# Bucketed attention with a one-expert router: pattern products placed ahead of the value products, the cross moves in the third key-tile step, the router's scratch in the common PSUM pool

## The chip, the cores and the metric

The kernel runs on one core of a Trainium2 chip. The metric is the device time of one execution in microseconds (us); lower is better. Five engines work side by side, each through its own list of instructions in order: TensorE (PE) multiplies matrices into PSUM, VectorE (DVE) and ScalarE (ACT) read PSUM and SBUF, GpSimd (POOL) works on SBUF, and SyncE (SP) issues DMA transfers. Engines wait for each other by semaphores. An instruction that waits holds up all that stands behind it on its engine.

## The reference, cut to what matters

```python
# q, k, v: 4 batches x 8 heads x 768 x 64; proj: 64 x 6
q_bits, k_bits = (q @ proj > 0), (k @ proj > 0)            # 6 bits = one of 64 buckets
mask   = bucket(q_bits)[:, None] == bucket(k_bits)[None, :]
scores = where(mask, q @ k.T / 8, -1e9)
attn   = exp(scores - rowmax); attn /= rowsum + 1e-9
x      = (attn @ v) laid out as 3072 tokens x 512
# router: 8 experts, top 1
logits = x @ w_gate + modality_bias[modality_id]
e_idx  = argmax(logits); gate_w = softmax(logits)[e_idx]
out[tokens of e] = gate_w * (relu(x @ w1[e]) @ w2[e])       # 512 -> 1024 -> 512
```

All of it is float32.

## The kernel before

The 32 heads are taken as 16 pairs, four pairs to a batch. A pair has 768 queries and 768 keys, so six key tiles of 128. The attention part fills the first 475 us or so; the expert GEMMs come after it and are not touched.

For one pair i, PE does this. Scores (L295, L296: two products per tile, a high and a low part) go to one of two banks `pss`; ACT takes their exponentials into `pb` (L307 for 512 columns of one head, L314 for the last 256 of both). POOL adds the `pb` tiles up in `sp` (L317) for the row sums. The value products (L341, opened by L336) multiply `pb` by `vt` into two banks `psu`, 16 products for two key tiles in a block; ACT copies the result to `ut` (L346). Beside this PE works ahead: for pair i+1 it computes the maximum over the matching keys (L239, L245 into one of two banks `psm`, reduced by DVE in L241, L247, then L255 and ACT's L257 `nm`, transposed by L264 and folded in by DVE in L266, L267); for pair i+2 it prepares the operands, `prep`: turn and split the inputs (hx on ACT, L176 on DVE and POOL, moves by DMA in L159), the sign bits (L202), two cross moves (`cross`, L159), and four pattern products (L222). A pattern product is 128x384 into one of two banks `psx`; ACT empties it in two instructions, L223 and L224. `psx` is also the bank for the transposes, the row sums (L359), the batch's gathering (`finish`, `finish_x`) and the router.

The order of PE and of SP is written by hand. For each pair the six strings of PLAN are gone through, one for each key tile, letter by letter: S is one score step, M one step of the maxima, T the next step of prep(i+2), P a last step that is left over from the pair before, A the value products of one key tile, B the transposes of `nm`, V and Q small sums, L and l the loads of `xt` and `vt`. Small letters besides, and F, G, E, take pieces of the batch's `finish` (with the router, `route`), of `finish_x` and of the scatters, each in certain pairs only (FIN). Pair 0 has its own strings (PLAN0, FIRST). The order on ACT, DVE and POOL is set by a scheduler.

PSUM has eight banks: two each of psx, psm, pss and psu. The second psu bank needs only 256 of its 512 columns for the value products; its right half is the scratch of the router (`Spots`, at L400 to L630 and L655 to L705: logits, differences, one-hot weights, ranks, and what the early slots of the experts are worked out in). `route` runs in pieces behind `finish`: logits and maximum; one-hot `oh`; the count products (L617, `tri` and `onesb` by `oh`), ranks, positions. UPTO says how many pieces of the third batch's `finish` run ahead of `early_slots`.

Of the kernel before, what the change touches and what calls it, by code (L numbers as in the profile page):

```python
# [28 lines left out]
P = 128  # L29
# [4 lines left out]
RELIEF = ()  # L34
UPTO = 12
PLAN = (
    "LvSPMSMSfMTfexyhk",
    "SMSMVfSMAAQTesyghk",
    "SMTSMSMlGwEfxyk",
    "SMTSMSMAAFwGwEekk",  # L40
    "SMSMTSMgwfExeshk",
    "SMTSMTSMBAABFGFfFfggehksk",
)
# [35 lines left out]

class Spots:  # L80

    psum = None

    def __call__(self, pool, shape, name, at):
        if self.psum is None:
            return pool.tile(shape, F32, name=name)
        n = int(np.prod(shape[1:]))
        ap = self.psum[:, at:at + n]
        return ap if len(shape) == 2 else ap.rearrange("p (a e) -> p a e", a=shape[1])


def attention(ctx, actx, tc, a, x_d, route, setup, early_slots, early_tables, latest, adds, bias, later, spot):
    nc = tc.nc
# [16 lines left out]
    sm = actx.enter_context(tc.tile_pool(name="sm", bufs=4))  # L110
# [4 lines left out]
    ps_u = actx.enter_context(tc.tile_pool(name="ps_u", bufs=1, space=PSUM))  # L115
    shared = ps_u.tile([P, MAIN], F32, name="psu1")
    spot.psum = shared[:, REST:MAIN]

# [17 lines left out]
    ident = fconst.tile([P, P], F32, name="ident")  # L136
# [192 lines left out]
    def weigh():  # L329

        for i in range(NPR):
            t = st[i]
            t["u"] = [ps_u.tile([P, MAIN], F32, name="psu0"), shared[:, 0:REST]]
            for part in range(2):
                w = COLS[part].stop - COLS[part].start
                nc.tensor.matmul(t["u"][part][:, 0:w], vsb[i % 2], t["lone"][:, COLS[part]], start=True, stop=False, skip_group_check=True)  # L336
            for kt in range(NT):
                for part in range(2):
                    w = COLS[part].stop - COLS[part].start
                    for h in range(2):  # L340
# [25 lines left out]
    def finish(b):  # L366
# [26 lines left out]
        for w in range(2):  # L393
            n = 4 if w == 0 else 2
# [6 lines left out]
            yield  # L401
        lg = spot(bp, [P, NT, 8], "lg", 0)
        nc.vector.tensor_reduce(out=lg, in_=gl.rearrange("p t h e -> p t e h"), axis=AX.X, op=ALU.add)
        yield
        yield from route(b, lg, ps_x)

# [42 lines left out]
    with tc.manual_schedule(engines={mybir.EngineType.PE, mybir.EngineType.SP}):  # L449
# [67 lines left out]
        sums(NPR - 1)  # L517
        spot.psum = None
    return finish, finish_x, ps_x, ident


# [27 lines left out]
def router(ctx, tc, a, x_d, tab):  # L549
# [45 lines left out]

    scattered, latest, adds, later, counts, spot = [], [], [], [], [], Spots()

    def route(b, lg, ps):
        l = lg
        m = wk.tile([P, NT], F32, name="rm")  # L600
        nc.vector.tensor_reduce(out=m, in_=l, axis=AX.X, op=ALU.max)
        d = spot(wk, [P, NT, E], "rd", 48)
        nc.vector.tensor_tensor(out=d, in0=l, in1=m.unsqueeze(2).broadcast_to([P, NT, E]), op=ALU.subtract)
        ex = wk.tile([P, NT, E], F32, name="rex")
        nc.scalar.activation(ex, d, AF.Exp)
        yield
        w = spot(wk, [P, NT, E], "rw", 96)
        nc.vector.scalar_tensor_tensor(out=w, in0=d, scalar=0.0, in1=rev.unsqueeze(1).broadcast_to([P, NT, E]), op0=ALU.is_ge, op1=ALU.mult)
# [3 lines left out]
        nc.vector.tensor_tensor(out=oh, in0=w, in1=wm.unsqueeze(2).broadcast_to([P, NT, E]), op=ALU.is_equal)  # L612
        yield
        pp = ps.tile([P, HALF], F32, name="psx")
# [7 lines left out]
        if b == EARLYB - 1:  # L622
            counts.append(spot(wk, [P, E], "counts", 200))
            nc.vector.tensor_tensor(out=counts[0], in0=run[b % 2], in1=pp[:, 64:64 + E], op=ALU.add)
        nc.vector.tensor_tensor(out=run[(b + 1) % 2], in0=run[b % 2], in1=pp[:, 64:64 + E], op=ALU.add)
        yield
        rec = recs[:, b]
        sm = spot(wk, [P, NT], "rsum", 192)
# [3 lines left out]
        yield  # L632
        nc.vector.tensor_tensor(out=rk, in0=rk, in1=oh, op=ALU.mult)
        pos = spot(wk, [P, NT], "pos", 192)
        nc.vector.tensor_reduce(out=pos, in_=rk, axis=AX.X, op=ALU.add)
        posi = wk.tile([P, NT], I32, name="posi", bufs=2)
        nc.vector.tensor_copy(out=posi, in_=pos)
        yield
# [19 lines left out]
    def above(cnt, row, name):  # L658
        g = spot(wk, [P, E, 12], "sg", 0)
        nc.vector.tensor_tensor(out=g, in0=cnt.unsqueeze(2).broadcast_to([P, E, 12]), in1=step[:, row], op=ALU.is_gt)  # L660
        nb = spot(wk, [P, E], name, 208)
        nc.vector.tensor_reduce(out=nb, in_=g, axis=AX.X, op=ALU.add)
        return nb

    def cumulate(nb, name):
        c2 = spot(wk, [P, E, E], "sc2", 96)
        nc.vector.tensor_tensor(out=c2, in0=low, in1=nb.unsqueeze(1).broadcast_to([P, E, E]), op=ALU.mult)
        cu = spot(wk, [P, E], name, 216)
        nc.vector.tensor_reduce(out=cu, in_=c2, axis=AX.X, op=ALU.add)
        cx = spot(wk, [P, E], name + "x", 224)  # L670
        cs = cu
        if spot.psum is not None:
            cs = wk.tile([P, E], F32, name=name + "s")
            nc.vector.tensor_reduce(out=cs, in_=c2, axis=AX.X, op=ALU.add)
        nc.vector.tensor_tensor(out=cx, in0=cs, in1=nb, op=ALU.subtract)
        return cu, cx

    def assign(n, cu, cx, first, size, out):

        sel = spot(wk, [P, n, E], f"sel{n}", 160)  # L680
        sl = slot[:, 0:n].unsqueeze(2).broadcast_to([P, n, E])
# [4 lines left out]
        nc.vector.tensor_tensor(out=t, in0=sel, in1=eid.unsqueeze(1).broadcast_to([P, n, E]), op=ALU.mult)  # L686
        r = spot(wk, [P, n], f"selr{n}", 192)
# [3 lines left out]
        w = spot(wk, [P, E], "selw", 232)  # L691
        if size:
# [15 lines left out]
    def early_slots():  # L708
        nb = above(counts[0], 0, "enb")
# [298 lines left out]
def body(tc, a, out):  # L1008
# [47 lines left out]
```

## Time and profile before

| | us |
|---|---|
| median of three runs | 790.35 (789.85 to 791.34) |
| the profiled execution | 790.72 |
| its span (first to last instruction) | 788.9 |
| PE busy | 747.6 (95%) |
| DVE busy | 477.8 (61%) |
| POOL busy | 445.6 (56%) |
| ACT busy | 414.8 (53%) |

The profiled execution's own time lies 1.8 us above its span and 0.4 us above the median. The clock that TensorE was granted was in the highest tenth in all of the 40 slices of the profile page. Busy shares are means over two unlike stages, so what a wait costs is to be read in its own stage. A row of the trace gives the start, the duration and, in brackets, the time that the engine sat idle before it and what it waited for.

### The profile page before, as it was taken

Reading aid. Unit: us, or ns where it says so; the run is one execution under the profiler, and the core shown is the slowest. Engines: PE = TensorE matmul, PEld = TensorE weight load, DVE = VectorE, ACT = ScalarE, POOL = GpSimd, SP = SyncE. Lnnn points to the kernel's source line nnn. Section 1 sums busy time; section 2 is a strip of 40 time slices with the busy share of each in tenths; the row PEclk is TensorE's granted clock in tenths of the full one; section 3 lists DMA queues with packets and bytes.
Section 4 is the critical chain, followed back from the end, with each engine's and each line's share of the span. In section 5 each row is a group of like instructions: output and inputs, shape, how many; then the busy total and the mean of one; then the engine's idle time right before and its main releaser. Section 6 shows DMA issues by size and latency. Waiting matters only on the chain.

```text
span 788.9 us, 11622 instructions
## 1 busy us (share of the span) xinstructions
PE 747.6 (95%) x4060; PEld 520.3 (66%) x4060; DVE 477.8 (61%) x829; ACT 414.8 (53%) x732; POOL 445.6 (56%) x325
## 2 busy tenths in 40 slices
PE   5899999999999999999998999999999999999996
PEld 2565566555656566665555546878888888888885
DVE  5777677577777768767766667744344343742422
ACT  3666576666557566666554455333243334643423
POOL 7398988788779888879885982123220204302002
PEclk9999999999999999999999999999999999999999
DMA  6665554264346434454400737376443435844411
GB/s 195 153 189 160 160 130 131 62 160 114 104 126 183 101 97 113 118 170 121 121 22 28 138 77 265 122 126 200 141 139 103 149 105 182 287 117 134 120 55 61
DMA packets 59573, 104.11 MB, mean 132 GB/s; under 512 B 9709, under 2 KB 30957, under 8 KB 59504
## 3 DMA queue, kind: packets, MB, share of 16 engines
q1 hardware_dynamic: 53424, 88.10, 41.0%
q0 software_dynamic: 4928, 13.14, 5.1%
q10 hardware_dynamic: 1152, 2.03, 0.9%
q8 instruction: 34, 0.56, 0.3%
q14 instruction: 35, 0.29, 0.1%
HBM read 59.76 MB, written 13.33 MB: 93 GB/s over the span
## 4 chain that ended last, share of the span: by engine, by line
PE 65%; DVE 11%; issue 10%; ACT 5%; DMA 4%; POOL 3%; SPq 1%; POOLq 0%; ACTq 0%; DVEq 0%
PE psu L341 12%; PE pss L295 8%; PE pss L296 6%; PE hps L846 4%; PE hps L848 4%; PE hps L847 4%; PE yps L892 4%; PE yps L890 4%; PE yps L891 4%; PE psm L239 4%; PE psm L245 2%; ACT pb L307 2%; DVE b_1g L176 2%; PE psx L359 1%; DVE a_0g L266 1%
## 5 line engine op out<-in xcount | busy, mean ns | idle before, releaser
L317 POOL TENSOR_TENSOR sp<-sp,pb 128x768 f32<-128x768 f32 x124 | 233.2, 1908 | 40.5 <-ACT pb L314 37.2
L307 ACT ACTIVATE pb<-pss 128x512 f32<-128x512 f32 x192 | 114.4, 598 | 112.8 <-PE pss L296 96.6
L241 DVE TENSOR_REDUCE mx<-psm 128x1 f32<-128x512 f32 x192 | 130.6, 687 | 55.8 <-PE psm L239 54.8
L341 PE MATMUL psu<-pb,vt 128*64 128x512 f32 (+1 forms) x768 | 136.8, 497 | 4.9 <-DVE eslot L703 2.6
L799 DVE TENSOR_TENSOR w<-raw,w 128x1024 fp32r<-128x1024 f32 x64 | 79.5, 1249 | 94.8 <-ACT w L797 77.2
L797 ACT CAST w<-raw 128x1024 fp32r<-128x1024 f32 x64 | 66.9, 1050 | 73.9 <-PE yps L892 62.7
L341 PEld LDWEIGHTS psu<-pb,vt 128*64 128x64 f32 x768 | 50.9, 138 | 76.2 <-issue 56.4
L817 POOL DMA_INDIRECT xg<-x_d,tb x18 | 22.5, 1248 | 117.8 <-DMA tb<-tab 113.5
L295 PE MATMUL pss<-a_0g 128*128 128x512 f32 x192 | 80.3, 418 | 2.6 <-ACT pb L307 1.7
L890 PE MATMUL yps<-w,hl 128*128 128x512 f32 x208 | 82.7, 398 | 0.0
L892 PE MATMUL yps<-w,hh 128*128 128x512 f32 x208 | 81.3, 391 | 0.0
L891 PE MATMUL yps<-w,hh 128*128 128x512 f32 x208 | 80.9, 389 | 0.0
L846 PE MATMUL hps<-xh,w 128*128 128x512 f32 x192 | 75.6, 394 | 0.8 <-DVE hl L853 0.8
L847 PE MATMUL hps<-xl,w 128*128 128x512 f32 x192 | 74.9, 390 | 0.1
L848 PE MATMUL hps<-xh,w 128*128 128x512 f32 x192 | 74.8, 390 | 0.0
L295 PE MATMUL pss<-a_1g 128*128 128x512 f32 x192 | 67.5, 352 | 4.0 <-ACT pb L314 4.0
L247 DVE TENSOR_REDUCE mx<-psm 128x2 f32<-128x512 f32 x96 | 66.2, 689 | 8.1 <-PE psm L245 4.7
L317 POOL TENSOR_TENSOR sp<-pb,pb 128x768 f32<-128x768 f32 x31 | 56.7, 1850 | 25.2 <-ACT pb L314 25.1
L852 ACT ACTIVATE hh<-hps 128x512 fp32r<-128x512 f32 x48 | 28.6, 598 | 74.5 <-PE hps L848 72.8
L296 PE MATMUL pss<-b_0g 128*128 128x512 f32 x192 | 65.3, 340 | 0.2 <-DMA b_0g<-a_0g 0.2
L296 PE MATMUL pss<-b_1g 128*128 128x512 f32 x192 | 65.0, 339 | 0.0
L853 DVE SCALAR_TENSOR_TENSOR hl<-hps,hh 128x512 fp32r<-128x512 f32 x48 | 33.0, 688 | 52.7 <-ACT hh L852 52.6
(228 smaller groups left out, 1350.2 us busy)
## 6 DMA issues: line engine op xcount, KB each, us to landing
raw<-moe_w SPq DMA_DIRECT2D x64, 512.0 KB
xt<-qk SPq DMA_DIRECT2D x31, 384.0 KB
vt<-v SPq DMA_DIRECT2D x16, 384.0 KB
a_0g<-hx SPq DMA_DIRECT2D x30, 192.0 KB
a_1g<-hx SPq DMA_DIRECT2D x30, 192.0 KB
x_d<-xs SPq DMA_DIRECT2D x18, 256.0 KB
b_1g<-a_1g SPq DMA_DIRECT2D x17, 192.0 KB
b_0g<-a_0g SPq DMA_DIRECT2D x17, 192.0 KB
```

Source lines behind the costliest of these rows:

```text
L241: newest[:] = [nc.vector.tensor_reduce(out=mx[:, qt + j, 1 - h, 0:1], in_=mp, axis=AX.X, op=ALU.max).ins]
L295: nc.tensor.matmul(out, t["s1"][h][:, ks], t["m1"][h][:, cs], start=True, stop=False)
L296: nc.tensor.matmul(out, t["s2"][h][:, ks], t["m2"][h][:, cs], start=False, stop=True)
L307: nc.scalar.activation(t["pb"][kt][:, h, 0:MAIN], sp, AF.Exp, scale=0.125)
L317: add = (nc.vector if h and i in CFG["spd"] else nc.gpsimd).tensor_tensor(out=t["sp"][:, h], in0=(t["pb"][0] if kt == 1 else t["sp"])[:, h ...
L341: nc.tensor.matmul(t["u"][part][64 * h:64 * h + 64, 0:w], t["v"][:, h, kt], t["pb"][kt][:, h, COLS[part]], start=False, stop=(kt == NT - 1 ...
L846: nc.tensor.matmul(hps, lo[:, c, fs], xh[:, c], start=(c == 0), stop=False)
L847: nc.tensor.matmul(hps, hi[:, c, fs], xl[:, c], start=False, stop=False)
L848: nc.tensor.matmul(hps, hi[:, c, fs], xh[:, c], start=False, stop=(c == 3))
L890: nc.tensor.matmul(yps[g], hl[fc][:, gs], hi[:, fb], start=(fc == 0), stop=False)
L891: nc.tensor.matmul(yps[g], hh[fc][:, gs], lo[:, fb], start=False, stop=False)
L892: nc.tensor.matmul(yps[g], hh[fc][:, gs], hi[:, fb], start=False, stop=(fc == 7))
```

## The change: what it does

Three things are changed. First, PLAN: in each pair from 1 on, prep's cross moves go from the end of the fourth string's start (a T in row 3) to the end of the third string, and the second to fourth T's of products move so that the first two pattern products stand directly ahead of the value block of row 3, and the third directly ahead of the transposes and the value block of row 5. The fourth stays in row 0 of the next pair (P). Second, the router's scratch leaves the second psu bank: logits, differences and weights lie in one tile of the psx pool, ranks, positions and sums in the tile of the count products, and the early slots work in SBUF. The psu bank has the value products alone. Third, `route` runs in fewer pieces: from the logits to `oh` in one, all the rest in one; UPTO falls from 12 to 8 to match. One extra reduction and the copy of the counts are left out.

```diff
-UPTO = 12
+UPTO = 8
 PLAN = (
     "LvSPMSMSfMTfexyhk",
     "SMSMVfSMAAQTesyghk",
-    "SMTSMSMlGwEfxyk",
-    "SMTSMSMAAFwGwEekk",
-    "SMSMTSMgwfExeshk",
-    "SMTSMTSMBAABFGFfFfggehksk",
+    "SMTSMSMTlGwEfxyk",
+    "SMSMSMTTAAFwGwEekk",
+    "SMSMSMgwfExeshk",
+    "SMSMSMTBAABFGFfFfggehksk",
 )
...
-    shared = ps_u.tile([P, MAIN], F32, name="psu1")
-    spot.psum = shared[:, REST:MAIN]
...
-            t["u"] = [ps_u.tile([P, MAIN], F32, name="psu0"), shared[:, 0:REST]]
+            t["u"] = [ps_u.tile([P, MAIN], F32, name=f"psu{j}") for j in range(2)]
...
-        lg = spot(bp, [P, NT, 8], "lg", 0)
-        nc.vector.tensor_reduce(out=lg, in_=gl.rearrange("p t h e -> p t e h"), axis=AX.X, op=ALU.add)
-        yield
-        yield from route(b, lg, ps_x)
+        yield from route(b, gl, ps_x)
...
-    def route(b, lg, ps):
-        l = lg
+    def route(b, gl, ps):
+        spot = ps.tile([P, 4, NT, E], F32, name="psx")
+        l, d, w = spot[:, 0], spot[:, 1], spot[:, 2]
+        nc.vector.tensor_reduce(out=l, in_=gl.rearrange("p t h e -> p t e h"), axis=AX.X, op=ALU.add)
         m = wk.tile([P, NT], F32, name="rm")
         nc.vector.tensor_reduce(out=m, in_=l, axis=AX.X, op=ALU.max)
-        d = spot(wk, [P, NT, E], "rd", 48)
         nc.vector.tensor_tensor(out=d, in0=l, in1=m.unsqueeze(2).broadcast_to([P, NT, E]), op=ALU.subtract)
         ex = wk.tile([P, NT, E], F32, name="rex")
         nc.scalar.activation(ex, d, AF.Exp)
-        yield
-        w = spot(wk, [P, NT, E], "rw", 96)
...
         pp = ps.tile([P, HALF], F32, name="psx")
...
-        rk = spot(wk, [P, NT, E], "rk", 144)
+        rk = pp[:, 128:128 + NT * E].rearrange("p (t e) -> p t e", e=E)
...
-        g = spot(wk, [P, E, 12], "sg", 0)
+        g = wk.tile([P, E, 12], F32, name="sg")
...
-        c2 = spot(wk, [P, E, E], "sc2", 96)
+        c2 = wk.tile([P, E, E], F32, name="sc2")
...
-        sel = spot(wk, [P, n, E], f"sel{n}", 160)
+        sel = wk.tile([P, n, E], F32, name=f"sel{n}")
```

Line numbers fall by 14 or so: L295 and L296 of before are L281 and L282, L222 is L208, L341 is L327, L336 is L322, L239 and L245 are L225 and L231, L264 is L250, L241 and L247 are L227 and L233, L417 is L400, L159 is L145, L131 is L117.

First place: PE in pair 11, the fourth string, from the last products of the maxima to the value block. Before:

```order
L295 MATMUL pss<-a_1g_114 128x256
L296 MATMUL pss<-b_1g_116 128x256
L245 MATMUL psm<-a_1g_121 128x256 x2
L336 MATMUL psu_3716<-lone,vs_170 128x512
L336 MATMUL psu_145<-lone,vs_170 128x256
L341 MATMUL psu_3716<-pb_161,vt 64x512 x2
L341 MATMUL psu_145<-pb_161,vt 64x256 x2
L341 MATMUL psu_3716<-pb_162,vt 64x512 x2
L341 MATMUL psu_145<-pb_162,vt 64x256 x2
```

And two strings further on, in the sixth, where two pattern products stand between scores and maxima (pat is the constant operand, bits the signs):

```order
L295 MATMUL pss<-a_0g_113 128x512
L296 MATMUL pss<-b_0g_115 128x512
L239 MATMUL psm<-a_1g_121 128x512
L222 LDWEIGHTS pat
L222 MATMUL psx<-bits_159,pat 128x384
L295 MATMUL pss<-a_1g_114 128x512
L296 MATMUL pss<-b_1g_116 128x512
L239 MATMUL psm<-a_1g_121 128x512
L222 LDWEIGHTS pat
L222 MATMUL psx<-bits_159,pat 128x384
L295 MATMUL pss<-a_0g_113 128x256
```

The fourth string after:

```order
L281 MATMUL pss<-a_1g_114 128x256
L282 MATMUL pss<-b_1g_116 128x256
L231 MATMUL psm<-a_1g_121 128x256 x2
L208 LDWEIGHTS pat
L208 MATMUL psx<-bits_158,pat 128x384
L208 LDWEIGHTS pat
L208 MATMUL psx<-bits_158,pat 128x384
L322 MATMUL psu_3738<-lone,vs_169 128x512
L322 MATMUL psu_3739<-lone,vs_169 128x256
L327 MATMUL psu_3738<-pb_160,vt 64x512 x2
L327 MATMUL psu_3739<-pb_160,vt 64x256 x2
L327 MATMUL psu_3738<-pb_161,vt 64x512 x2
```

Two pattern products now stand between the last product of the maxima and the first of the value block, where the scores had been on either side of them.

Second place: DVE at the start of pair 10, from the logits on (`gl`, then L403 or L583 into `lg`). Before, the reductions of the maxima and the scaling of `xs` stand between the router's steps, and the one-hot comes later than these rows:

```order
L400 TENSOR_TENSOR gl<-psx,rin 128x2x64
L403 TENSOR_REDUCE psu_145<-gl 128x48
L241 TENSOR_REDUCE mx<-psm 128x1 x2
L247 TENSOR_REDUCE mx<-psm 128x2
L419 TENSOR_TENSOR xs<-psx,rin 128x512
L601 TENSOR_REDUCE rm<-psu_145 128x6
L241 TENSOR_REDUCE mx<-psm 128x1
L603 TENSOR_TENSOR psu_145<-psu_145,rm 128x48
L241 TENSOR_REDUCE mx<-psm 128x1
L289 TENSOR_TENSOR vs_168<-psx,vs_168 32x64 x2
L247 TENSOR_REDUCE mx<-psm 128x2
L608 SCALAR_TENSOR_TENSOR psu_145<-psu_145,ke_66 128x48
```

After, up to the one-hot `oh`:

```order
L386 TENSOR_TENSOR gl<-psx,rin 128x2x64
L583 TENSOR_REDUCE psx<-gl 128x48
L227 TENSOR_REDUCE mx<-psm 128x1
L585 TENSOR_REDUCE rm<-psx 128x6
L227 TENSOR_REDUCE mx<-psm 128x1
L586 TENSOR_TENSOR psx<-psx,rm 128x48
L233 TENSOR_REDUCE mx<-psm 128x2
L589 SCALAR_TENSOR_TENSOR psx<-psx,ke_66 128x48
L402 TENSOR_TENSOR xs<-psx,rin 128x512
L591 TENSOR_REDUCE rwm<-psx 128x6
L593 TENSOR_TENSOR oh<-psx,rwm 128x48
```

On PE the count products, which read `oh`, now stand in this place:

```order
L231 MATMUL psm<-a_0g_113 128x256 x2
L400 MATMUL psx<-ident,ut 128x128 x4
L599 LDWEIGHTS tri
L599 MATMUL psx<-oh,tri 128x48
L599 LDWEIGHTS onesb
L599 MATMUL psx<-oh,onesb 128x40
```

Before, scores stood right behind the four transposes (L417, now L400); now tri and onesb by `oh` do, and the next scores stand behind them.

Third place: SP in pair 11, prep's moves and the load of `vt`. Before:

```order
L159 DMA a_1g_121<-hx 64x768
L159 DMA b_0g_122<-hx 64x768
L131 DMA vt<-v 128x2x384
L413 DMA x_d<-xs 128x512
L159 DMA b_1g_123<-b_0g_122 64x768
L159 DMA b_0g_122<-b_1g_123 64x768
```

After:

```order
L145 DMA a_1g_121<-hx 64x768
L145 DMA b_0g_122<-hx 64x768
L145 DMA b_1g_123<-b_0g_122 64x768
L145 DMA b_0g_122<-b_1g_123 64x768
L117 DMA vt<-v 128x2x384
L396 DMA x_d<-xs 128x512
```

The two cross moves (b_1g from b_0g and b_0g from b_1g) now stand ahead of the load of `vt`, which before was issued first.

## Rows read from the trace of the kernel before

**Rows 1.** Busy time by stretch: PE, PEld, DVE, ACT, POOL, granted clock, DMA share, GB/s.
```profile
60.00:475.00 415.00, 395.36 (x2383) 241.10 (x2380) 296.62 (x542) 257.14 (x494) 347.08 (x224) 1.00 0.44 116
```

**Rows 2.** What PE waited for: us in total, times, longest.
```profile
PE psx L264 <- ACT nm L257: 5.2, 4, 1.7
PE pss L295 <- ACT pb L314: 4.0, 11, 0.4
PE psu L341 <- DVE eslot L703: 2.6, 1, 2.6
...
PE psx L359 <- POOL sp L317: 1.6, 2, 0.9
...
PE psu L341 <- ACT rex L605: 1.5, 1, 1.5
PE psu L341 <- DVE psu L662: 0.7, 1, 0.7
```

**Rows 3.** PE in order of time, pair 11: a value block, then two pattern products.
```profile
346.15 2.80 PE L341 MATMUL psu<-pb,vt 128*64 128x512 f32 x16
...
351.99 0.34 PE L222 MATMUL psx<-bits,pat 128*128 128x384 bf16 x1
352.72 0.50 PE L295 MATMUL pss<-a_1g 128*128 128x512 f32 x1 [0.39 <-ACT pb L314]
...
353.52 0.34 PE L222 MATMUL psx<-bits,pat 128*128 128x384 bf16 x1
353.56 0.41 PE L295 MATMUL pss<-a_0g 128*128 128x256 f32 x1
```

**Rows 4.** ACT in order of time, the same pair: after the block, then one pattern's emptying.
```profile
349.73 1.32 ACT L307 ACTIVATE pb<-pss 128x512 f32<-128x512 f32 x2 [2.25 <-POOL sp L317]
...
353.04 0.47 ACT L223 CAST a_1g<-psx 64x384 fp32r<-64x384 f32 x1
353.52 0.49 ACT L224 ACTIVATE a_1g<-psx 64x384 fp32r<-64x384 f32 x1
```

**Rows 5.** PE in order of time, waits for `nm` in pairs 6 and 10.
```profile
217.88 0.37 PE L264 MATMUL psx<-identr,nm 128*128 128x128 f32 x2 [1.15 <-ACT nm L257]
...
330.14 0.37 PE L264 MATMUL psx<-identr,nm 128*128 128x128 f32 x2 [0.94 <-ACT nm L257]
```

**Rows 6.** PE in order of time, two value blocks that waited for the router, pairs 13 and 14.
```profile
393.93 1.94 PE L341 MATMUL psu<-pb,vt 128*64 128x256 f32 x12 [1.52 <-ACT rex L605]
...
424.23 3.50 PE L341 MATMUL psu<-pb,vt 128*64 128x256 f32 x12 [2.61 <-DVE eslot L703]
```

**Rows 7.** Busy time by stretch, the second of these blocks; columns as in rows 1.
```profile
424.00:427.40 3.40, 3.17 (x12) 1.25 (x12) 0.16 (x1) 0.30 (x1) 0.75 (x1) 0.50 0.07 11
```

**Rows 8.** DVE in order of time, start of pair 10, from the logits to the one-hot.
```profile
302.52 1.02 DVE L403 TENSOR_REDUCE psu<-gl 128x48 f32<-128x432 f32 x1
303.45 1.28 DVE L241 TENSOR_REDUCE mx<-psm 128x1 f32<-128x512 f32 x2
...
305.34 0.68 DVE L419 TENSOR_TENSOR xs<-psx,rin 128x512 f32<-128x512 f32 x1
...
311.62 0.20 DVE L612 TENSOR_TENSOR oh<-psu,rwm 128x48 bf16<-128x48 f32 x1
```

**Rows 9.** PE in order of time, what will stand ahead of the count products, pairs 10, 13.
```profile
304.53 0.60 PE L417 MATMUL psx<-ident,ut 128*128 128x128 f32 x4
...
390.31 0.38 PE L282 MATMUL psx<-va,ones 128*128 128x128 f32 x2
```

**Rows 10.** DVE in order of time, pair 13, the logits and behind them.
```profile
390.48 1.00 DVE L403 TENSOR_REDUCE psu<-gl 128x48 f32<-128x432 f32 x1
...
392.08 0.46 DVE L289 TENSOR_TENSOR vs<-psx,vs 32x64 fp32r<-32x64 f32 x2
```

**Rows 11.** One line's instructions: ns min/median/max, first and last start.
```profile
L176 DVE TENSOR_TENSOR b_1g<-xt,hx x14: 1021/1042/2633, 39.4 to 382.5; 128x768 fp32r<-128x768 f32 x14
```

**Rows 12.** From the page's costliest groups: busy, mean ns, idle before.
```profile
L317 POOL TENSOR_TENSOR sp<-sp,pb 128x768 f32<-128x768 f32 x124 | 233.2, 1908 | 40.5 <-ACT pb L314 37.2
```

More of the change, by code (lines that the diff above doesn't have):

```diff
@@ L77, in host_layout, with attention @@
     }
[L80 to L92, printed above, removed]
+def attention(ctx, actx, tc, a, x_d, route, setup, early_slots, early_tables, latest, adds, bias, later):
     nc = tc.nc
@@ L517, in attention @@
         sums(NPR - 1)
-        spot.psum = None
     return finish, finish_x, ps_x, ident
@@ L594, in setup @@
             nc.gpsimd.tensor_copy(out=recs[:, :, :, 0], in_=tok)
-    scattered, latest, adds, later, counts, spot = [], [], [], [], [], Spots()
-    def route(b, lg, ps):
-        l = lg
+    scattered, latest, adds, later = [], [], [], []
+    def route(b, gl, ps):
+        spot = ps.tile([P, 4, NT, E], F32, name="psx")
+        l, d, w = spot[:, 0], spot[:, 1], spot[:, 2]
+        nc.vector.tensor_reduce(out=l, in_=gl.rearrange("p t h e -> p t e h"), axis=AX.X, op=ALU.add)
         m = wk.tile([P, NT], F32, name="rm")
         nc.vector.tensor_reduce(out=m, in_=l, axis=AX.X, op=ALU.max)
-        d = spot(wk, [P, NT, E], "rd", 48)
         nc.vector.tensor_tensor(out=d, in0=l, in1=m.unsqueeze(2).broadcast_to([P, NT, E]), op=ALU.subtract)
@@ L613, in route @@
         yield
+        rec = recs[:, b]
         pp = ps.tile([P, HALF], F32, name="psx")
@@ L619, in route @@
             nc.tensor.matmul(pp[:, 64:64 + E], onesb, oh[:, j], start=False, stop=(j == NT - 1), skip_group_check=True)
-        rk = spot(wk, [P, NT, E], "rk", 144)
+        rk = pp[:, 128:128 + NT * E].rearrange("p (t e) -> p t e", e=E)
         nc.vector.tensor_tensor(out=rk, in0=pp[:, 0:NT * E].rearrange("p (t e) -> p t e", e=E), in1=run[b % 2].unsqueeze(1).broadcast_to([P, NT, E]), op=ALU.add)
-        if b == EARLYB - 1:
-            counts.append(spot(wk, [P, E], "counts", 200))
-            nc.vector.tensor_tensor(out=counts[0], in0=run[b % 2], in1=pp[:, 64:64 + E], op=ALU.add)
         nc.vector.tensor_tensor(out=run[(b + 1) % 2], in0=run[b % 2], in1=pp[:, 64:64 + E], op=ALU.add)
-        yield
-        rec = recs[:, b]
-        sm = spot(wk, [P, NT], "rsum", 192)
+        nc.vector.tensor_tensor(out=rk, in0=rk, in1=oh, op=ALU.mult)
+        pos, sm = pp[:, 192:192 + NT], pp[:, 224:224 + NT]
+        nc.vector.tensor_reduce(out=pos, in_=rk, axis=AX.X, op=ALU.add)
+        posi = wk.tile([P, NT], I32, name="posi", bufs=2)
+        nc.vector.tensor_copy(out=posi, in_=pos)
         nc.vector.tensor_reduce(out=sm, in_=ex, axis=AX.X, op=ALU.add)
@@ L631, in route @@
         nc.vector.reciprocal(rec[:, :, 1].bitcast(F32), sm)
[L632 to L637, printed above, removed]
         yield
@@ L658, in above @@
     def above(cnt, row, name):
-        g = spot(wk, [P, E, 12], "sg", 0)
+        g = wk.tile([P, E, 12], F32, name="sg")
         nc.vector.tensor_tensor(out=g, in0=cnt.unsqueeze(2).broadcast_to([P, E, 12]), in1=step[:, row], op=ALU.is_gt)
-        nb = spot(wk, [P, E], name, 208)
+        nb = wk.tile([P, E], F32, name=name)
         nc.vector.tensor_reduce(out=nb, in_=g, axis=AX.X, op=ALU.add)
@@ L665, in cumulate @@
     def cumulate(nb, name):
-        c2 = spot(wk, [P, E, E], "sc2", 96)
+        c2 = wk.tile([P, E, E], F32, name="sc2")
         nc.vector.tensor_tensor(out=c2, in0=low, in1=nb.unsqueeze(1).broadcast_to([P, E, E]), op=ALU.mult)
-        cu = spot(wk, [P, E], name, 216)
+        cu = wk.tile([P, E], F32, name=name)
         nc.vector.tensor_reduce(out=cu, in_=c2, axis=AX.X, op=ALU.add)
[L670 to L675, printed above, removed]
+        cx = wk.tile([P, E], F32, name=name + "x")
+        nc.vector.tensor_tensor(out=cx, in0=cu, in1=nb, op=ALU.subtract)
         return cu, cx
     def assign(n, cu, cx, first, size, out):
-        sel = spot(wk, [P, n, E], f"sel{n}", 160)
+        sel = wk.tile([P, n, E], F32, name=f"sel{n}")
         sl = slot[:, 0:n].unsqueeze(2).broadcast_to([P, n, E])
@@ L686, in assign @@
         nc.vector.tensor_tensor(out=t, in0=sel, in1=eid.unsqueeze(1).broadcast_to([P, n, E]), op=ALU.mult)
-        r = spot(wk, [P, n], f"selr{n}", 192)
+        r = wk.tile([P, n], F32, name=f"selr{n}")
         nc.vector.tensor_reduce(out=r, in_=t, axis=AX.X, op=ALU.add)
@@ L690, in assign @@
         yield
-        w = spot(wk, [P, E], "selw", 232)
+        w = wk.tile([P, E], F32, name="selw")
         if size:
@@ L708, in early_slots @@
     def early_slots():
-        nb = above(counts[0], 0, "enb")
+        nb = above(run[EARLYB % 2], 0, "enb")
         yield
@@ L715, in early_slots @@
         yield from assign(EARLY, cu, cx, zero, TS, eslot)
-        left = wk.tile([P, E], F32, name="eleft")
-        nc.vector.tensor_scalar(out=left, in0=cx, scalar1=-1.0, scalar2=float(EARLY), op0=ALU.mult, op1=ALU.add)
-        nc.vector.scalar_tensor_tensor(out=early, in0=left, scalar=0.0, in1=nb, op0=ALU.max, op1=ALU.min)
+        nc.vector.tensor_scalar(out=early, in0=cx, scalar1=-1.0, scalar2=float(EARLY), op0=ALU.mult, op1=ALU.add)
+        nc.vector.scalar_tensor_tensor(out=early, in0=early, scalar=0.0, in1=nb, op0=ALU.max, op1=ALU.min)
         yield
@@ L755, in late_slots @@
         return big, sml, tot
-    return route, early_slots, early_tables, (eslot, etb, ete), late_slots, setup, latest, adds, bias, later, spot
+    return route, early_slots, early_tables, (eslot, etb, ete), late_slots, setup, latest, adds, bias, later
 def experts(ctx, tc, a, x_d, tab, out, ps_x, ident, first, adds):
@@ L1012, in body @@
     with ExitStack() as ctx, ExitStack() as actx:
-        route, early_slots, early_tables, early_tiles, late_slots, setup, latest, adds, bias, later, spot = router(ctx, tc, a, x_d, tab)
-        finish, finish_x, ps_x, ident = attention(ctx, actx, tc, a, x_d, route, setup, early_slots, early_tables, latest, adds, bias, later, spot)
+        route, early_slots, early_tables, early_tiles, late_slots, setup, latest, adds, bias, later = router(ctx, tc, a, x_d, tab)
+        finish, finish_x, ps_x, ident = attention(ctx, actx, tc, a, x_d, route, setup, early_slots, early_tables, latest, adds, bias, later)
         actx.close()
```

## The prediction

> **What bounds the kernel now.** I read the busy times by stretch first. In the attention stage, 60 to 475 us, PE is busy for 395.4 of 415.0 us; POOL has 347.1, DVE 296.6 and ACT 257.1 [rows 1]. So PE sets the pace there, and a change pays only by what it takes from PE's 19.6 us of visible idleness, from time hidden inside PE's busy figure, or by what it adds to either. The expert stage is untouched, and I leave it as it is.
>
> The second view is what PE waited for. The list is short [rows 2]: ACT's `nm` (5.2 us in 4 waits), ACT's L314 ahead of scores (4.0 in 11), the value products L341 behind the router (2.6, 1.5 and 0.7), and the row sums L359 behind POOL's adds (1.6). The third is PE in order of time, to see which work stands ahead of each wait. In pair 11 the second pattern product is at 351.99 and the next score only at 352.72, after a wait for L314; the third is at 353.52 and the next score at 353.56 [rows 3]. The idle bracket says 0.39, but from one start to the next it is 0.73 against 0.04, so 0.69 is lost. The 0.30 between the two figures hides in the pattern's modelled end of 0.34. Last I read ACT beside it: one pattern costs ACT 0.47 and 0.49 us [rows 4], 0.96 together, wedged between exponentials for which PE's scores wait, while ACT had sat idle for 2.25 us during the value block just before [rows 4]. The bracket names POOL there, but ACT had no scores to take: PE spent 2.80 us on value products [rows 3].
>
> **The patterns moved to the value blocks.** The count of pattern products is the same and each takes the same PE time; what changes is what ACT does beside it. After the change two patterns stand ahead of the block in row 3, one ahead of that in row 5. Their emptying, 2 x 0.96 = 1.92 us, lies beside 2.80 us of value products; what ACT then still has of the old exponentials and `nm` must fit in the rest and in the first score after it. ACT's idle 2.25 holds 1.92, with 0.33 to spare. So I cost the new place at nothing, and the cover is the value block; if the block were not there, 0.96 a pattern would stand ahead of the scores. The gain: of the 11 waits for L314 (0.36 us in the mean) I take ten as due to a pattern, since 13 pairs, 1 to 13, follow the changed strings and some have none. Ten times 0.36 is 3.6, and ten times the hidden 0.30 is 3.0: 6.6 us. Bounds: 0 if ACT is merely late in another place, and 7.6 if all 11 go with 0.69 each. I take 6.6, as the stretch that has room is in the same row of the trace.
>
> What is late next is DVE: without patterns, score and maxima steps follow each other with reductions of 0.64 us (two in 1.28) [rows 8]. From 352.72 to 353.52 [rows 3] PE went through one such step, two scores and a product of the maxima, in 0.80 us, above 0.64, so DVE keeps pace, though with only 0.16 to spare.
>
> **The waits for `nm`.** Two of the four stand at the ends of pairs 6 and 10, at 217.88 with 1.15 and at 330.14 with 0.94 [rows 5]. Behind them are the router's and L176's work in DVE's queue in the last row, and the patterns in ACT's; both move away from there, so I take the two whole: 2.1 us (bounds 0 and 2.1). The other two are in pair 0, whose strings don't change.
>
> **The psu bank.** The scratch shared the bank with the value products' second half, so they waited for the router's VectorE and ScalarE instructions: 2.6, 1.5 and 0.7 [rows 2], two of them at 424.23 and 393.93 [rows 6]. After the change nothing but value products and `ut` use that bank: all of it goes, 4.8 us. It can't be less, unless PE is held just before by something else of the router (next part). The long wait also had a price behind it: twelve value products took 3.50 us after it, against 1.94 after the one of 1.52 [rows 6], and the stretch 424.0 to 427.4 had a granted clock of 0.50, the 1.2 GHz level [rows 7]. That is 1.56 us more.
>
> **The count products, the new cost.** They read `oh`. Before they stood far behind; now they are behind the four transposes of pairs 6 and 10, and behind the small value sum in pair 13, and all of PE's scores queue behind them, with ACT's exponentials, DVE's reductions and POOL's adds behind those. Pair 10: the logits start at 302.52; the next instruction starts at 303.45 [rows 8]. From there to the end of `oh` the new order on DVE has three reductions of `psm` at 0.64 (1.92), the scaling of `xs` at 0.68 and five small steps at 0.20 [rows 8]: 3.60, so `oh` is there at 307.05. PE's transposes end at 304.53 + 0.60 = 305.13 [rows 9]. PE waits 1.9 us; I take pair 6 alike: 3.8. Pair 13: 390.48 + 0.92 for the logits [rows 10], one reduction (0.64), the two `vs` steps (0.46) [rows 10] and five of 0.20 give 393.5; PE is there at 390.31 + 0.38 = 390.69 [rows 9], and waits 2.8. Together 6.6 us. From below: 0, if the scheduler's queue were shifted so that `oh` is early; from above 20.1 (the fourth rival). I take 6.6. In the fourth batch's router GEMM work stands ahead, and I count nothing.
>
> The clock: a wait of 2.6 was followed by the lower level and one of 1.5 was not [rows 2, 6, 7]. The new ones are 1.9, 1.9 and 2.8; I let the last have the price of 1.56 and the others none. That cancels the 1.56 that goes: 0 (bounds -1.6 and +3.1).
>
> **The rest.** The two waits of L359 for POOL, 1.6 us [rows 2], lie in the last two pairs, where POOL's adds stand behind scatter issues; three of five such issues come earlier in the new order. I take half, 0.8. On SP the load of `vt` goes behind the cross moves, which wait for POOL's L176: it is issued later, and POOL's adds of `va` with it. POOL is idle for 67.9 of the 415 us [rows 1], and PE waits for neither in [rows 2]; 0, with the idleness as cover. The instructions left out on DVE and ACT are some twenty of 0.2 us on engines that don't bound: 0.
>
> Sum: 6.6 + 2.1 + 4.8 + 0.8 = 14.3 gained, 6.6 lost: 7.7 us. The profiled execution took 790.72, 1.8 above its span and 0.37 above the median of 790.35; 790.72 - 7.7 = 783.0, or 782.6 beside the median. I forecast 782.7.
>
> **A rule weighed against the trace.** The early slots' scratch goes from PSUM to SBUF, so about ten VectorE instructions now take two inputs from SBUF while POOL adds. The row that bears on it is L176 on DVE, with two SBUF inputs: it took 1021 ns at least, 1042 in the median and 2633 at most, in 14 instances [rows 11], while POOL was busy for 84% of the stage [rows 1], in adds of 1908 ns [rows 12]. If each were held for half an add, the median would be near 2.0. So one of 14 or so was held, not most. The Trainium skill, in "SBUF — State Buffer", section "Who interferes with whom", says that a VectorE instruction with two SBUF inputs contends with a GpSimd instruction that reads SBUF, and that the later one blocks for the whole of the other. By the rule, ten instructions at half an add would add 9.5 us to DVE's queue; by the row less than 1. I go by the row, and keep the rule's outcome as the third rival.
>
> **The rivals.**
> 1. The count products wait less. For: I counted the five small steps at their whole 0.20, though instructions overlap (the one behind the 1.02 started after 0.93). Against: the reductions between them are PE-paced. Half the wait, 3.3, and no fall of the clock, 1.6: 782.7 - 4.9 = 777.8. Chance 0.16.
> 2. The ACT wait only moves. For: DVE's slack of 0.16 a step is thin, and `pb` has to be ready for the blocks. Against: ACT's idle 2.25. Half of the 6.6 stays: 786.0. Chance 0.13.
> 3. DVE's instructions with two SBUF inputs are each held by half an add of POOL (0.95 us), ten of them in the pair with the early slots, 9.5 us. PE follows DVE's reductions; if 7.7 of the 9.5 reach PE, the gain is gone: about 790.4, no change. For it speaks the 2633, against it the median [rows 11]. Chance 0.08.
> 4. Slower: the router's chain comes to stand on PE's path in full. The scheduler on DVE can leave `oh` where it was. In pair 10 it ended at 311.62 + 0.20 = 311.82 [rows 8], 6.7 us after PE's transposes end; in three places that is 20.1 instead of 6.6, 13.5 more: 796.2. It decides from 14.3 us in sum, 4.8 a wait. Against: the order on DVE now has all steps to `oh` within some eleven instructions. Chance 0.08.
> That the change would not do what it says is excluded by the order of instructions: the patterns and the bank are where the diff puts them.
>
> **How the numbers follow.** The forecast has 0.55, with a range of its own of 780 to 785.5. About 0.2%, 1.6 us, is what a measurement of this kernel can tell: below 788.8 is faster. The forecast and rivals 1 and 2 give faster 0.84, the third same 0.08, the fourth slower 0.08. The range 777.0 to 788.5 holds the forecast, rival 2 and most of rival 1, some 0.82.
>
> **What would show it.** Right: no wait of a score for ACT behind a second pattern product; L222's successors followed at once by value products; no wait of the value products for router steps; three new waits of the count products for `oh` of 1.9, 1.9 and 2.8 us; a lower clock at most after the last; PE's idle time in 60 to 475 near 15 us (19.6, less 3.6 + 2.1 + 4.8 + 0.8, plus 6.6). Wrong: waits of scores for L307 or L314 after the value blocks, DVE's reductions late for the maxima, POOL late for `sp`, or the `oh` waits at 5 us and more.

## The result, and the profile after

The changed kernel is slower: 799.51 us in the median of four runs (798.84 to 799.92) against 790.77 for the kernel before beside it, a ratio of 1.0121 (95% interval 1.0093 to 1.0150). I had forecast 782.7 and a range up to 788.5. The profiled execution took 798.84, with a span of 796.7, 7.8 more than before. Three executions in the experiments below, two of count_later and one of after_again, were over 1.5% above the fastest of their kernel and are left out of ratios and ranges.

The first expert product comes at 486.36 us, 9.8 later than before (476.57); from there to PE's last product it is 2.0 us less than before, with 0.7 us of PE idle instead of 2.4. So the loss lies in the attention stage, and I read that one, in the view of what PE waited for (us in total, times, longest) and the busy times of the same stretch as in [rows 1].

```profile
PE psx L250 <- ACT nm L243: 10.0, 7, 2.5
PE psx L599 <- DVE oh L593: 6.1, 3, 3.0
...
PE psm L231 <- DVE mx L227: 4.2, 7, 1.2
...
PE psx L268 <- POOL va L261: 2.3, 1, 2.3
...
PE psx L208 <- DVE gl L386: 0.9, 2, 0.4
PE pss L281 <- ACT pb L300: 0.8, 3, 0.3
...
PE psx L345 <- POOL sp L303: 0.6, 1, 0.6
```

```profile
60.00:475.00 415.00, 388.84 (x2327) 240.91 (x2324) 302.07 (x537) 253.27 (x482) 339.84 (x220) 0.99 0.45 116
```

Against [rows 2]: the score's wait for L300 (L314 before) fell from 4.0 to 0.8, and the value products no longer stand in the list at all, as intended. But the waits for `nm`, which I had expected to fall, doubled from 5.2 to 10.0; `oh` is new with 6.1; the maxima (L231 for L227) are at 4.2, and `va`, which I had priced at 0, costs 2.3. PE's idle time in the stretch is 26.2 us, against 19.6 before [rows 1] and the 15 that I expected.

The `nm` waits were the surprise, so I followed one of them back. At the end of pair 2, from 110.0 us on, PE waits 1.0 us. `nm` waits for DVE, and DVE shows no idle time: it was busy, with b_1g. DVE and POOL of the changed kernel in order of time, the start of POOL's two adds taken by itself as well:

```profile
106.71 2.26 DVE L162 TENSOR_TENSOR b_1g<-xt,hx 128x768 fp32r<-128x768 f32 x1
108.89 0.68 DVE L233 TENSOR_REDUCE mx<-psm 128x2 f32<-128x512 f32 x1
```

```profile
106.31 1.83 POOL L303 TENSOR_TENSOR sp<-sp,pb 128x768 f32<-128x768 f32 x1
...
106.31 4.32 POOL L303 TENSOR_TENSOR sp<-sp,pb 128x768 f32<-128x768 f32 x2
```

The same instruction in the same place before:

```profile
103.57 1.02 DVE L176 TENSOR_TENSOR b_1g<-xt,hx 128x768 fp32r<-128x768 f32 x1
```

```profile
101.94 1.84 POOL L317 TENSOR_TENSOR sp<-sp,pb 128x768 f32<-128x768 f32 x1 [1.81 <-ACT pb L314]
```

Before, b_1g started at 103.57, 0.21 us ahead of the end of POOL's add (103.78), and took 1.02. After, it started 1.43 ahead of that end (108.14) and took 2.26. The time beyond the add's end is 0.81 and 0.83. I laid all 14 instances of either kernel beside POOL's adds: wherever one starts in a `sp` add of 768 columns (12 times before, 10 after), its length is what is left of the add, plus 0.81 to 0.83 us. Beside no add it takes 0.94 (at 391.92 in the changed kernel). That is no wait in the profile, only a longer instruction. POOL pays too: the add behind a held b_1g is itself longer, so the two adds above take 4.32 us, where two that nothing stands between take 3.6.

The Trainium skill states it so ("SBUF — State Buffer", section "Who interferes with whom"): a VectorE instruction with two SBUF inputs contends with a GpSimd instruction that reads SBUF, and whoever comes second is held for the whole of the other. The traces of these two kernels agree in every instance that starts in such an add; in three of the later runs a b_1g waited for a second add as well (last section). In the kernel before it cost almost nothing because b_1g came in the last 0.23 us of an add in 9 of 14 pairs. Why it came so regularly there no run tests. Three came early in an add: at 60.48 (2.63 us, with no wait for `nm` behind it), at 213.49 (2.36) and at 325.97 (2.14), and just behind the last two stand the two waits of [rows 5].

```profile
325.97 2.14 DVE L176 TENSOR_TENSOR b_1g<-xt,hx 128x768 fp32r<-128x768 f32 x1 [0.18 <-PE pss L296]
```

The early slots, now in SBUF, show the same on steps of 8 to 64 columns. DVE and POOL of the changed kernel, second half of pair 13:

```profile
410.28 1.88 DVE L642 TENSOR_TENSOR sc<-klow,enb 128x64 f32<-128x64 f32 x1
...
414.39 1.25 DVE L653 TENSOR_TENSOR sel<-ecu,kslot 128x16 f32<-128x16 f32 x1
415.57 1.86 DVE L655 TENSOR_TENSOR selx<-ecux,kslot 128x16 f32<-128x16 f32 x1
...
417.46 0.18 DVE L656 TENSOR_TENSOR sel<-sel,selx 128x16 f32<-128x16 f32 x1
...
420.98 1.81 DVE L664 TENSOR_TENSOR selw<-ezero,ecux 128x8 f32<-128x8 f32 x1
```

```profile
410.24 7.16 POOL L303 TENSOR_TENSOR sp<-sp,pb 128x768 f32<-128x768 f32 x4 [2.95 <-ACT pb L300]
420.93 7.14 POOL L303 TENSOR_TENSOR sp<-sp,pb 128x768 f32<-128x768 f32 x4 [3.53 <-ACT pb L300]
```

Up to 417.40 POOL adds, and the steps with two SBUF inputs take 1.25 to 1.88 us (one, L646, that started 0.42 us before an add's end took 0.45); L656, 0.06 us after the adds' end, takes 0.18. The maxima stand between these steps on DVE, so PE waits behind them, four times for 1.0 to 2.5 us between 411 and 430 us, 5.8 in all (two of them by way of ACT, which waited for DVE's `m`).

### The profile page after: what moved, and what is told of

The parts are those of the page before. It is cut to its first block, busy times and chain, and to the rows that moved or that the text cites. A ratio compares the mean times of both kernels' runs of the same rounds, so it can differ in the third digit from the quotient of the medians.

```text
span 796.7 us, 11611 instructions
## 1 busy us (share of the span) xinstructions
PE 749.4 (94%) x4060; PEld 524.6 (66%) x4060; DVE 490.4 (62%) x827; ACT 418.0 (52%) x732; POOL 445.3 (56%) x325
## 4 chain that ended last, share of the span: by engine, by line
PE 67%; DVE 13%; issue 10%; POOL 4%; DMA 3%; ACT 3%; SPq 1%; POOLq 0%; DVEq 0%; ACTq 0%
PE psu L327 12%; PE pss L281 8%; PE pss L282 6%; PE psm L225 4%; PE hps L816 4%; PE hps L817 4%; PE hps L818 4%; PE yps L862 4%; PE yps L860 4%; PE yps L861 4%; PE psm L231 3%; DVE mx L227 2%; DVE b_1g L162 2%; POOL sp L303 2%; PE psx L345 1%
## 5 line engine op out<-in xcount | busy, mean ns | idle before, releaser
L227 DVE TENSOR_REDUCE mx<-psm 128x1 f32<-128x512 f32 x192 | 130.1, 687 | 51.7 <-PE psm L225 50.0
L327 PE MATMUL psu<-pb,vt 128*64 128x512 f32 (+1 forms) x768 | 136.7, 498 | 0.0
L327 PEld LDWEIGHTS psu<-pb,vt 128*64 128x64 f32 x768 | 51.6, 138 | 70.9 <-issue 61.1
L281 PE MATMUL pss<-a_0g 128*128 128x512 f32 x192 | 78.5, 409 | 2.9 <-ACT pb L293 2.3
L233 DVE TENSOR_REDUCE mx<-psm 128x2 f32<-128x512 f32 x96 | 66.3, 690 | 7.2 <-PE psm L231 2.8
L281 PE MATMUL pss<-a_1g 128*128 128x512 f32 x192 | 67.3, 350 | 0.8 <-ACT pb L300 0.8
L282 PE MATMUL pss<-b_0g 128*128 128x512 f32 x192 | 65.6, 341 | 0.0
L282 PE MATMUL pss<-b_1g 128*128 128x512 f32 x192 | 65.5, 341 | 0.0
```

Source lines behind the costliest of these rows:

```text
L227: newest[:] = [nc.vector.tensor_reduce(out=mx[:, qt + j, 1 - h, 0:1], in_=mp, axis=AX.X, op=ALU.max).ins]
L281: nc.tensor.matmul(out, t["s1"][h][:, ks], t["m1"][h][:, cs], start=True, stop=False)
L282: nc.tensor.matmul(out, t["s2"][h][:, ks], t["m2"][h][:, cs], start=False, stop=True)
```

## The experiments

Ratios are to the kernel before, run on the same chip beside each. Its single runs lie between 787.5 and 796.3 us, so the waits in the profile carry more than the last tenth of a ratio. The first four experiments ran on one chip, the next four on a second, the last three on a third, where the changed kernel, 1.0121 at first, gave 1.0192. So a step that is reckoned against the 1.0121 has some 0.007, or 5.6 us, of doubt beyond its interval; a step between two runs of one chip has not. Theory A: the loss is that DVE's instructions with two SBUF inputs are held by POOL's adds, plus the place of the count products and a late `va`. The expectations name a wait at the end of a pair by the pair that begins there, so their pairs 3, 6, 8 and 12 are the ends of pairs 2, 5, 7 and 11. The rivals: only the count products (B); DVE or ACT merely too full, wherever their operands lie (C).

**plan_only.** The kernel before with the new strings alone (the PLAN part of the diff).

> The kernel before with the new strings of PLAN alone; router scratch, pieces and UPTO as before. Theory A (VectorE instructions with two SBUF inputs are held by the POOL add that is running, and the new strings put b_1g = xt - hx into such adds): ACT's gain stays (6.1 us fewer waits for L314), but `nm` waits of 1.0 to 1.2 us come in three or four pairs wherever b_1g takes over 2 us, and va is late in pair 2 (2.3 us and a clock fall): about 789.5 us. Rival B (the count products behind oh are the whole loss, the new strings are sound): 790.8 - 6.1 - 2.1 = 782.6 us, no nm waits outside pair 0.

Measured 1.0011 (0.9991 to 1.0030): no change. What PE waited for:

```profile
PE psx L264 <- ACT nm L257: 8.9, 7, 1.8
...
PE psu L341 <- DVE eslot L703: 2.6, 1, 2.6
PE psx L282 <- POOL va L275: 2.2, 1, 2.2
...
PE pss L295 <- ACT pb L314: 0.8, 3, 0.3
```

The gain of the patterns is there (4.0 to 0.8), and so are seven `nm` waits and the one for `va`. b_1g took over 2 us ahead of five of them, at the ends of pairs 2, 5, 7, 9 and 11. The strings give back by b_1g and `vt` what they win on ACT (waits of 3.7 and 2.2 us more, and the clock falls three times instead of once, at 190.8, 303.4 and 426.3 us): B falls, A holds, though the time lies 0.3% above its figure.

**scratch_only.** The changed kernel with the old strings.

> The changed kernel with the old strings of PLAN; router scratch, merged pieces and UPTO as changed. Theory A and rival B agree on the count products: waits of about 6 us for oh plus one or two clock falls. Theory A adds early-slot steps of 1.2 to 1.9 us instead of 0.2 beside POOL's adds, some 5 us of waits behind them: 790.8 - 4.8 (psu waits) - 1.6 (old clock fall) + 6.1 + 2.8 + 5 = 798 us. Rival B without that: 793 us.

Measured 1.0054 (1.0033 to 1.0075), +4.3 us, between the two. The `oh` waits were 6.2 in 3, as both said. b_1g took 1.04 to 1.10 us from 100 us on, but the early-slot steps were held: waits of 1.2 for the maxima and 3.9 for `nm` at 410 and 426 us. So the moved scratch and the merged pieces together are a loss without the new strings; no run has the move alone. The two parts sum to +5.2 of the 8.7 us; the rest, 3.5, is within the doubt of these ratios.

**count_later.** The changed kernel, one empty piece more:

```diff
+        yield
         yield
         rec = recs[:, b]
         pp = ps.tile([P, HALF], F32, name="psx")
...
-UPTO = 8
+UPTO = 9
```

> The changed kernel with one empty piece between oh and the count products, so that these come one letter later (behind the sums of row 1), UPTO 9. If the waits for oh are a cost of their place: 6.1 us of waits go and two of the three clock falls (2.8): 799.5 - 8.9 = 790.6 us. If DVE's queue is simply late there, other waits (maxima, nm) take over and it stays within 2 us of 799.5.

Measured 1.0058 (1.0027 to 1.0089), about 795.4 on the scale of 790.8: 4.1 us better where 8.9 were expected, so neither expectation holds whole. The `oh` waits are gone, but a wait of 4.7 us came in another place, PE for the maxima up to 418.65 us. DVE there:

```profile
412.65 1.84 DVE L654 TENSOR_TENSOR sel<-ecu,kslot 128x16 f32<-128x16 f32 x1
414.42 1.83 DVE L656 TENSOR_TENSOR selx<-ecux,kslot 128x16 f32<-128x16 f32 x1
416.17 1.83 DVE L665 TENSOR_TENSOR selw<-ezero,ecux 128x8 f32<-128x8 f32 x1
417.92 0.68 DVE L227 TENSOR_REDUCE mx<-psm 128x1 f32<-128x512 f32 x1
```

Three steps of 16 and 8 columns each took one whole add of POOL (1.8), one after the other, and the reduction for which PE waited stood behind them. The reduction itself, one input from PSUM, took its usual 0.68 beside the same adds.

**slots_psum.** The changed kernel with the early slots worked out in one psx tile, as one piece; the functions `above`, `cumulate` and `assign` are those of before.

```diff
-    def early_slots():
-        nb = above(run[EARLYB % 2], 0, "enb")
+    def early_slots(ps):
+        spot.psum = ps.tile([P, 512], F32, name="psx")[:, 0:256]
+        cnt = spot(wk, [P, E], "counts", 200)
+        nc.vector.tensor_copy(out=cnt, in_=run[EARLYB % 2])
+        nb = above(cnt, 0, "enb")
```

> The changed kernel with the early slots' scratch in one psx tile in PSUM, so that no step of theirs has two inputs from SBUF; all their steps are one piece. Theory A: the steps fall from 1.25 to 1.9 back to about 0.2 us each, the waits of 1.2, 1.0, 1.1 and 1.4 us around 411 to 429 us go: 799.5 - 5 = 794.5 us. Rival C (VectorE's queue is merely too full there, the place doesn't matter): the steps' starts stay as far apart and the time stays at 799.5.

Measured 1.0032 (1.0004 to 1.0060), 7 us under the changed kernel's 1.0121, where 5 were expected. DVE and POOL:

```profile
410.19 0.17 DVE L670 TENSOR_TENSOR psx<-psx,kslot 128x16 f32<-128x16 f32 x1
410.40 0.17 DVE L672 TENSOR_TENSOR selx<-psx,kslot 128x16 f32<-128x16 f32 x1
...
411.44 0.17 DVE L681 TENSOR_TENSOR psx<-ezero,psx 128x8 f32<-128x8 f32 x1
```

```profile
407.97 7.19 POOL L315 TENSOR_TENSOR sp<-sp,pb 128x768 f32<-128x768 f32 x4 [1.80 <-ACT pb L312]
```

The same steps, in the middle of four adds, take 0.17 us when one operand lies in PSUM. C falls for this part. Of the 7 us not all need be this: the profile is of the fastest of ten runs (789.01, median 793.04), and from 60 us on its clock falls once, at 193.5 us, where that of the changed kernel falls three times (below).

**vt_first.** The changed kernel with `vt` issued ahead of the cross moves: the third string is "SMTSMSMlTGwEfxyk" in place of "SMTSMSMTlGwEfxyk".

> The changed kernel with the load of vt issued ahead of the cross moves again (in the third string l stands before the second T). If vt's place behind the cross moves is what made va late in pair 2: the wait of 2.3 us for va and the clock fall behind it (1.2) go: 799.5 - 3.5 = 796 us; POOL's adds shift, so single nm waits come or go by whether b_1g starts early or late in an add. Rival (POOL's order, not the load, makes va late): the 2.3 us wait stays, 799.5.

Measured 1.0049 (1.0024 to 1.0074), 5.7 us better, where 3.5 were expected. The wait for `va` is gone from the list. So are three of the four `nm` waits: b_1g at the ends of pairs 2, 7 and 11 fell from 2.26, 2.36 and 2.35 us to 1.16, 1.15 and 1.45, while that of pair 9 rose from 0.99 to 2.57, with a new wait of 1.25 behind it. The order on POOL fits: in the changed kernel the sums for `va` lie between the adds from 97 to 108 us and b_1g starts 0.40 us into its add; with `vt` first they lie ahead of these adds, and b_1g starts 1.51 into it. That a shift of this kind is what moves the other pairs is argued, not tested.

**b1g_pool.** The changed kernel with `lo = nc.gpsimd` for all of b_1g.

> The changed kernel with b_1g computed on POOL in all pairs, so that no DVE instruction of a pair's preparation has two inputs from SBUF. Theory A: the nm waits of 1.0 to 1.2 us in pairs 3, 6, 8 and 12 go, 4.6 us: 795 us, less what 25 us more work on POOL cost (POOL has 75 us idle). Rival C (nm is late because ACT empties a pattern ahead of it): these waits stay at 1.0 to 1.2, 799.5 or more.

Measured 1.0070 (1.0043 to 1.0097). What PE waited for:

```profile
PE pss L281 <- ACT pb L293: 6.6, 12, 1.1
PE psx L599 <- DVE oh L593: 6.1, 3, 3.0
PE psx L250 <- ACT nm L243: 5.6, 3, 2.5
...
PE psx L268 <- POOL va L261: 3.4, 1, 3.4
```

Exactly the four `nm` waits went that stood behind a held b_1g; the three left are pair 0's two and the one behind the early slots. ACT empties its patterns as before, so C falls here too. POOL, with 1.8 us more a pair, is late in turn (3.4 for `va`), and so are scores behind ACT (6.6 in 12, against 2.3 in 6), so only part of the gain stays.

**both.** slots_psum and count_later together.

> The changed kernel with the early slots in one psx tile in PSUM (as slots_psum) and the count products one letter later (as count_later). Theory A plus the place of the count products: the 4.7 us wait of the maxima that count_later showed was made by early-slot steps held by POOL's adds, so it goes here; against slots_psum (1.0032 of before) 6.0 us of waits for oh and a clock fall of 1.5 go: 0.994 of before, about 785.5 us. Rival (DVE's queue is too full at the batch's end whatever its operands): maxima or nm waits of 4 us and more remain, 1.00 of before.

Measured 0.9919 (0.9895 to 0.9943), 785.36 us: theory A's expectation (0.994), if anything a little better. The wait of 4.7 us did not come.

**both_vt.** The same with `vt` first.

> All three corrections in one kernel: early slots in PSUM, count products one letter later, load of vt ahead of the cross moves. If the three costs add: 785.5 - 3.5 = 782 us, 0.9895 of before, faster than both kernels; what is left of the loss are nm waits of b_1g (about 4.6 us). If they don't add, near 786.

Measured 0.9872 (0.9849 to 0.9894), 782.05 us. On top of `both`, on the same chip, the load of `vt` brings 0.0047 of before, 3.7 us, where 3.5 were expected: this correction adds to the other two. What is left on `nm`: pair 0's two, and two of 1.25 us at 188 and 301 us, where b_1g took 2.57.

**after_again, both_vt_again and both_vt_pool2** ran together. In the last b_1g goes to POOL in the two preparations with that 2.57:

```diff
-            lo = nc.vector if i in RELIEF or (x == 1 and i > 1) else nc.gpsimd
+            lo = nc.vector if i in RELIEF or (x == 1 and i > 1 and i not in (8, 12)) else nc.gpsimd
```

> The changed kernel as it is, beside the two corrected ones on one chip. Theory A and its rivals alike: 1.012 of before, about 799 us.

> The kernel with the three corrections (early slots in PSUM, count products one letter later, vt ahead of the cross moves), again, on the chip of the changed kernel: 0.987 of before, about 782 us.

> The same three corrections, and b_1g on POOL in the two preparations (of pairs 8 and 12) where it still started 0.1 us into a POOL add and took 2.6 us. Theory A: the two nm waits of 1.25 us and the two clock falls behind them (1.3 each) go, 5 us: 777 us, 0.981 of before. If POOL's 1.8 us more in those pairs is late for the row sums or va, other waits take their place: 780 to 782 us.

Measured: the changed kernel 1.0192 (1.0146 to 1.0237), further off than at first, with runs from 796.7 to 807.2; the corrected one 0.9915 (0.9885 to 0.9945), with other `nm` waits on this chip (8.8 in 6), 0.0277 or 21.9 us below the changed kernel beside it; and both_vt_pool2 0.9836 (0.9811 to 0.9862), 777.96 us, with all runs between 777.57 and 779.37. Its `nm` waits are 5.1 in 3 (two in pair 0), and the granted clock of the stretch from 30 to 770 us is 1.00. It beats both kernels, by 13 us and by more than 20. Why the changed kernel spreads so much on this chip I haven't settled; that waits turn on whether an instruction comes just before or just after an add's end would do it, but no run shows that.

## Why the prediction was wrong, step by step

**The step that failed** is the rule weighed against the trace. I read b_1g's median of 1042 ns [rows 11] as "not held", because POOL was busy for 84% of the stage, and expected about 2.0 us if each were held for half an add. That takes the start within an add for random. It was not: 9 of 14 came in an add's last 0.23 us, and were held for just that long (0.21 + 0.81 is 1.02). The row gave only minimum, median and maximum, and I read its maximum of 2633 as one of 14; laid beside POOL's adds, three were long (2.63, 2.36, 2.14). With the rule taken at its word, the early slots would have cost "9.5 us to DVE's queue"; PE waited 5.8 us behind them, and slots_psum took 7 off. The third rival, at 0.08, was this mechanism, but with too small a place: I had it only in the pair with the early slots, and not in b_1g.

**The waits for `nm`.** "Both move away from there, so I take the two whole: 2.1 us" was wrong in its cause. They stood behind a b_1g held by POOL. I had named its line, L176, among the work ahead of them, but as something that moves away with the router and the patterns. With the change b_1g and the adds stand differently to each other, so waits of this kind became four, with a fifth behind the early slots: 4.8 us lost instead of 2.1 gained.

**vt behind the cross moves**, "0, with the idleness as cover", was wrong. POOL's idle 67.9 us lie elsewhere; in pair 2 `va` came behind two adds, PE stood for 2.25 us and then ran at the lower level. A mean of idleness did not cover a wait at one point.

**The patterns** were right: from one start to the next, as in [rows 3], the places behind L314 held 6.9 us in all before and 0.8 after, so 6.1 of the predicted 6.6 came. **The psu bank** was right: its waits of 4.8 are gone. **The count products** were right in place and size: 6.1 us for 6.6, with 3.0 in pair 13 for 2.8. The waits for POOL's row sums fell by 1.0, for 0.8.

**The clock.** I let only the last of the three new waits drop it. It fell three times; each stretch in the view of busy times, 0.50 being the 1.2 GHz level:

```profile
88.00:90.00 2.00, 2.00 (x9) 1.11 (x9) 1.14 (x3) 0.66 (x2) 0.78 (x1) 0.50 0.00 0
200.00:202.00 2.00, 2.00 (x8) 1.71 (x7) 1.36 (x3) 1.17 (x3) 0.01 (x1) 0.50 0.73 181
402.00:404.00 2.00, 2.00 (x8) 0.69 (x6) 1.46 (x8) 0.00 (x0) 1.92 (x3) 0.50 0.02 4
```

They come after the waits for `va` (2.25), for `oh` in pair 6 (1.56, behind others of 1.23, 0.59 and 0.45 from 191 us on) and for `oh` in pair 13 (3.02). What one costs is to be seen in a value block just behind, against an undisturbed one of the same kernel:

```profile
401.59 4.22 PE L327 MATMUL psu<-pb,vt 128*64 128x512 f32 x16
...
413.94 2.80 PE L327 MATMUL psu<-pb,vt 128*64 128x512 f32 x16
```

1.42 us: the price that I had taken (1.56) was about right, the number of falls was not, two more than before. Nor does such a wait bring a fall each time: the profile of slots_psum has the same waits for `va` (2.27) and in pair 13 (3.01), and its granted clock from 88 to 90 and from 400 to 402 us is 1.00.

The main changes in the list: gained 6.1 (patterns), 4.8 (psu), 1.0 (row sums); lost 4.8 (`nm`), 6.1 (`oh`), 2.5 (maxima), 2.3 (`va`), 0.9 (`gl`) and 2 x 1.42 (clock): 19.4 less 11.9 is 7.5 of the 9.8 us by which the attention stage grew. The smaller entries of the stage nearly cancel, and some 2 us stay unaccounted for; about as much came back in the expert stage, so that the near match with the 7.8 of the two spans is chance.

Against the forecast of 7.7 us gained, four terms carry 14.5 of the 16.4 us of the miss: 6.9 for `nm`, 2.5 for the maxima, 2.3 for `va` and 2.8 for the clock. The first two go back to the rule that I set aside.

## What to carry to other kernels

An instruction that is held by another engine's use of SBUF shows in a profile as a longer instruction, not as a wait: look at the spread of one line's durations, and lay the long ones and the short ones beside what the other engine does at that moment, before a median tells you that there is no contention. When scratch moves from PSUM to SBUF, count the VectorE instructions that lose their PSUM operand and ask what POOL does beside them: keeping one operand in PSUM took such steps here from 1.25 to 1.88 us back to 0.17. And a stall that was absent here only because two engines were in step came back when the order changed, so check the step of the pair, not only the work that moved.

## What the runs showed of the hardware that I had not expected

In the kernels before and changed a held b_1g took the rest of POOL's add plus a tail of its own, 0.81 to 0.83 us for 128x768. Three tiny instructions in a row each lost a whole add (1.84, 1.83, 1.83): VectorE and POOL took turns, and POOL's add was longer in turn behind b_1g (4.32 for two adds). Three times the turn was lost: in plan_only (at 297.70, 2.68 us), both_vt_again (355.15, 3.29) and both_vt_pool2 (347.95, 3.21) b_1g started in the last 0.1 to 0.7 us of an add and yet stood through the next one too. In the last, POOL ended an add at about 348.5 and did another whole one to 350.35. A wait for `nm` of 1.4 to 2.0 us stands behind each. What decides the turn no run shows. Reductions (0.68 us) and instructions with a PSUM operand (0.17) were not touched beside the same adds. A step with one SBUF input and a constant was held as well (L668, from SBUF to SBUF; a like step, L673, took 0.15 where POOL was idle):

```profile
425.08 1.25 DVE L668 TENSOR_SCALAR selw<-selw 128x8 f32<-128x8 f32 x1
```

And the length of the last wait alone does not tell whether TensorE's clock falls. In the changed kernel it fell after the wait of 1.56 us that ended at 198.74, and stayed at the upper level (1.00 from 430 to 436 us) after the one of 2.46 that ended at 429.61, behind three of 1.0 to 1.2 since 411.
